# K one batch row further ahead of V in a decode-attention kernel: load order, P V step and buffers moved together

## The chip, the core and the metric

The kernel runs on one core of one Trainium2 chip. The metric is device time in microseconds (us), from the start to the end of one execution; a lower number is better. The profile is one further execution, recorded by the hardware profiler. Its span, from the first to the last instruction, is a little shorter than the device time of the same execution.

The core has five instruction streams that run side by side and meet only through semaphores: TensorE (PE; the weight loads that go with its matmuls are listed as PEld), VectorE (DVE), ScalarE (ACT), GpSimd (POOL) and SyncE (SP). Here SP only issues transfers. Sixteen DMA engines carry them out. Matmul results land in PSUM, all other on-chip data is in SBUF.

## What is computed

One decode step of a transformer layer for 8 batch rows, one token each: a layer norm, attention over the last 2048 positions of a cache, an output projection, and then a small MLP on the sum.

```python
# x: (8, 1, 512); k_cache, v_cache: (8, 8, 8192, 128) bf16; 32 query heads, 8 kv heads
def _A_ref(x, k_cache, v_cache, wq, wo):
    W = 2048                                   # min(4096, max(256, 8192 // 4))
    q = (x @ wq).reshape(8, 1, 32, 128).transpose(0, 2, 1, 3)
    k = jnp.repeat(k_cache[:, :, 8192 - W:, :], 4, axis=1)
    v = jnp.repeat(v_cache[:, :, 8192 - W:, :], 4, axis=1)
    scores = jnp.einsum("bhqd,bhkd->bhqk", q, k) * (128 ** -0.5)
    p = softmax(scores, axis=-1)
    o = jnp.einsum("bhqk,bhkd->bhqd", p, v)
    return o.transpose(0, 2, 1, 3).reshape(8, 1, 4096) @ wo

h  = x + _A_ref(layernorm(x), k_cache, v_cache, wq, wo)
h2 = h + _B_ref(layernorm(h), ...)             # layernorm, gelu(. @ w3) @ w4; the token shift is zero for one token
```

For each batch row the kernel reads 4 MB (in units of 2^20 bytes) of K and 4 MB of V, 64 MB in all, and beside them wq and wo (4 MB each) and the MLP's w3 and w4 (1.75 MB each).

## The kernel before

**Units.** One batch row of K (or V) comes in two transfers of 2 MB, called quads here: quad (k, b, j) holds four kv heads of row b. A *step* p handles a quarter of a quad: `split(i)` turns a step's number into row b = i // 8, quad j and quarter cq. So a row is 8 steps, and 8 rows are 64 steps (`NG`).

**The ring.** All K and V quads go through `ring`, a buffer of 8 slots (`NS`). The list `loads` (lines 235 to 242) gives their order: first row 0 of K, then row 1 of K, then wo, and from there one row of V and one row of K in turn. Quad number n in this list uses slot n % 8. SP issues the transfers in the order of the list (lines 430 to 457), and each waits until the quad eight places before it has been read by PE (`taken`): a K quad by the transposes of its last quarter, a V quad by the P V matmuls of its last quarter. w3 and w4 follow in the places 32 and 33, under the same rule. As SP is one stream, a transfer that waits holds back all behind it.

**A step.** The loop at line 388 writes out the order of PE by hand. In step p PE does: 16 transposes of K (`pe_T`, line 270), whose result ACT and DVE copy from PSUM to SBUF, half each (`evict`, lines 279 and 281); a piece of the softmax of an earlier row, if one is due; the P V matmuls of step p - `LPV` (`pe_PV`, line 360), 16 of them with 16 columns; and the score matmuls of step p - `LQK` (`pe_QK`, line 290). With `LPV` = 16, step p of row b works on V of row b - 2.

**The softmax of row b** starts when its last scores are there, in step 8b + 9: the maximum over a row of scores (`softmax_1`, DVE, line 299), its spread over the heads by two small PE matmuls with DVE work between them (`softmax_2` and `softmax_3`, lines 303 to 316), exp with the row sum on ACT (line 317), the expansion of P by a mask (line 325, on POOL, in the last row on DVE), four groups of transposes of P on PE (`softmax_4`, line 335), each copied to `pT_sb` by DVE (line 340), and the inverse of the sums into `rL` (`softmax_5`, lines 348 and 349). `softmax_5(b)` is called in step 8b + 16, just ahead of the first P V step of row b. `pT_sb` and `rL` have two buffers each, so rows b and b - 2 share one.

**The end.** After 64 steps with transposes come 16 without (`NG + LPV` = 80 in all). In steps 64 to 71 run the P V of row 6 and the softmax of row 7; in steps 72 to 79 the P V of row 7, then `scale` (line 369: times `rL`), the output projection in two halves (`pe_wo`, lines 379 and 383), and the MLP (lines 467 to 532). The last quad of V is loaded in four pieces with a semaphore each, so that the P V of a quarter can start when that quarter has landed. P V adds up in one PSUM tile, `oT_ps`, for all rows (the last half row uses `kbank[1]`); the first P V of a row waits until the row before has been scaled out of it.

## Time and profile before

| | us |
|---|---|
| device time, median of 3 runs | 209.04 (208.78 to 209.84) |
| device time of the profiled execution | 208.47 |
| its span | 206.7 |
| TensorE busy | 162.9 (79% of the span) |
| VectorE busy | 82.5 (40%) |
| ScalarE busy | 79.5 (38%) |
| GpSimd busy | 32.2 (16%) |

The transfers from HBM are 79.18 MB (here in units of 10^6 bytes), 383 GB/s over the span. The times of single instructions, the clock and the state of the DMA engines over the span stand in the prediction, each where it is used. A row of the chain of waits or of the timeline reads: start in us, duration in us, engine and line, what is written and read, and how many instructions were merged. In brackets stands how long the engine was idle before it and what ended that. A row of the DMA issues ends with the time from the issue of a transfer to its landing.

### The profile page before, as it was taken

What the parts mean: (1) busy time and instruction counts of PE and PEld (TensorE: products, weight loads), DVE (VectorE), ACT (ScalarE), POOL (GpSimd) and SP (SyncE); (2) the same over time, 40 slices, a digit from 0 to 9 for tenths busy, and PEclk for the clock granted to TensorE, in tenths of its full rate; (3) what the DMA queues carried; (4) which work ended last, traced back from release to release, by engine and by line L of the source; (5) the groups of instructions that cost most, each with busy time, mean ns of one, the idle gap of its engine ahead of it and who ended that gap; (6) DMA issues with size and microseconds to landing.
All of it is one profiled execution on the core that took longest, in us unless ns stands there. A gap on an engine that the chain in (4) does not pass through costs nothing.

```text
span 206.7 us, 6192 instructions
## 1 busy us (share of the span) xinstructions
PE 162.9 (79%) x2861; PEld 125.2 (61%) x2861; DVE 82.5 (40%) x197; ACT 79.5 (38%) x91; POOL 32.2 (16%) x38
## 2 busy tenths in 40 slices
PE   0047999970059999996999599989996999758885
PEld 0047666540057787784878386867784776457884
DVE  7303545450014346434344425356344444463022
ACT  5002756830013554552355135535552463030021
POOL 7000000430000340070007000700430061000000
PEclk9999999996556999999699969999999999955555
DMA  7999999999999999999999999999999999996000
GB/s 293 419 403 406 453 406 373 383 450 414 444 419 438 422 434 422 428 431 425 431 428 427 431 428 428 431 428 428 431 425 431 428 428 420 405 423 265 17 3 2
DMA packets 10249, 79.57 MB, mean 385 GB/s; under 512 B 744, under 2 KB 4848, under 8 KB 6000
## 3 DMA queue, kind: packets, MB, share of 16 engines
q1 hardware_dynamic: 10208, 79.18, 91.3%
q8 instruction: 22, 0.36, 0.6%
q14 instruction: 3, 0.02, 0.0%
q10 hardware_dynamic: 16, 0.01, 0.0%
HBM read 79.18 MB, written 0.01 MB: 383 GB/s over the span
## 4 chain that ended last, share of the span: by engine, by line
PE 45%; DMA 36%; SPq 12%; DVE 5%; issue 1%; ACT 0%
DMA ring<-in_A_k_cache_dram 30%; PE kT_ps L270 17%; SPq L174 12%; PE S_ps L290 9%; PE oT_ps L360 7%; DMA wbig<-in_A_wq_dram 6%; PE sm L335 2%; PE S_ps L383 2%; PE S_ps L221 2%; PE kT_ps L486 2%; DVE pT_sb L340 1%; DVE P_sb L325 1%; PE sm L348 1%; PE kT_ps L360 1%; PE S_ps L523 1%
## 5 line engine op out<-in xcount | busy, mean ns | idle before, releaser
L279 ACT ACTIVATE kT_sb<-kT_ps 128x1024 bf16<-128x1024 bf16 x64 | 65.4, 1024 | 95.4 <-PE kT_ps L270 95.3
L270 PEld LDWEIGHTS kT_ps<-ident_b,ring 128*128 128x128 bf16 x1024 | 61.8, 102 | 47.3 <-DMA ring<-in_A_k_cache_dram 23.0
L270 PE MATMUL kT_ps<-ident_b,ring 128*128 128x128 bf16 x1024 | 72.8, 228 | 21.5 <-DMA ring<-in_A_k_cache_dram 21.5
L281 DVE COPY kT_sb<-kT_ps 128x1024 bf16<-128x1024 bf16 x64 | 44.3, 692 | 87.8 <-PE kT_ps L270 87.8
L325 POOL TENSOR_TENSOR P_sb<-P_sb,mask_b 128x512 bf16<-128x512 bf16 x28 | 28.2, 1041 | 138.4 <-ACT P_sb L317 138.4
L290 PE MATMUL S_ps<-kT_sb,qwin 128*32 128x512 bf16 x256 | 39.9, 610 | 0.0
L360 PE MATMUL oT_ps<-pT_sb,ring 128*128 128x16 bf16 x960 | 33.1, 171 | 0.0
L360 PEld LDWEIGHTS oT_ps<-pT_sb,ring 128*128 128x128 bf16 x960 | 31.0, 99 | 2.1 <-issue 2.0
L335 PE MATMUL sm<-ident_b,P_sb 128*128 128x128 bf16 x128 | 13.2, 230 | 3.4 <-DVE pT_sb L340 1.6
L340 DVE COPY pT_sb<-sm 128x512 bf16<-128x512 bf16 x32 | 13.4, 418 | 4.7 <-PE sm L335 4.7
L335 PEld LDWEIGHTS sm<-ident_b,P_sb 128*128 128x128 bf16 x128 | 8.6, 102 | 7.4 <-issue 4.1
L317 ACT ACTIVATE P_sb<-S_ps,negcol 128x512 bf16<-128x512 f32 x8 | 5.5, 688 | 7.7 <-DVE negcol L316 7.7
L221 PE MATMUL S_ps<-xlnT,wbig 128*128 128x8 bf16 x128 | 3.6, 168 | 6.2 <-DMA wbig<-in_A_wq_dram 6.2
L290 PEld LDWEIGHTS S_ps<-kT_sb,qwin 128*32 128x32 bf16 x256 | 6.7, 93 | 2.5
L221 PEld LDWEIGHTS S_ps<-xlnT,wbig 128*128 128x128 bf16 x128 | 3.5, 104 | 6.3 <-issue 6.3
L498 ACT ACTIVATE s<-vsum,eps 128x8 f32<-128x8 f32 x1 | 0.3, 301 | 17.1 <-DVE vsum L495 17.1
L299 DVE TENSOR_REDUCE mcol<-S_ps 128x1 f32<-128x512 f32 x8 | 5.5, 690 | 3.3 <-PE S_ps L290 3.3
L211 PE MATMUL sm<-ident_b,xln_b 8*128 8x8 bf16 x4 | 0.3, 174 | 6.5 <-DVE xln_b L195 6.5
L348 PE MATMUL sm<-lsel,ones_f 128*128 128x32 f32 x16 | 3.6, 314 | 1.3 <-DVE lsel L344 1.3
L228 DVE TENSOR_SCALAR qwin<-S_ps 128x32 bf16<-128x32 f32 x8 | 0.9, 182 | 9.2 <-PE S_ps L221 9.2
L348 PEld LDWEIGHTS sm<-lsel,ones_f 128*128 128x128 f32 x16 | 3.1, 241 | 1.8 <-DVE lsel L344 1.8
L211 PEld LDWEIGHTS sm<-ident_b,xln_b 8*128 8x128 bf16 x4 | 0.2, 114 | 6.5 <-DVE xln_b L195 6.5
(71 smaller groups left out, 74.5 us busy)
## 6 DMA issues: line engine op xcount, KB each, us to landing
ring<-in_A_k_cache_dram SPq DMA_DIRECT2D x16, 2048.0 KB, 23.8
ring<-in_A_v_cache_dram SPq DMA_DIRECT2D x15, 2048.0 KB, 18.9
wbig<-in_A_wq_dram SPq DMA_DIRECT2D x1, 4096.0 KB, 12.1
wbig<-in_A_wo_dram SPq DMA_DIRECT2D x4, 1024.0 KB, 17.0
ring<-in_A_v_cache_dram SPq DMA_DIRECT2D x4, 512.0 KB, 24.4
ring<-in_B_w_dram SPq DMA_DIRECT2D x1, 1792.0 KB, 21.9
ring<-in_B_w_dram SPq DMA_DIRECT2D x1, 1280.0 KB, 16.6
ring<-in_B_w_dram SPq DMA_DIRECT2D x1, 512.0 KB, 16.0
```

The costliest lines, as they stand in the source:

```text
L174: e.dma_start(dst, src).then_inc(sem, 16)
L221: ins = e.matmul(S_ps[0][:, h * B:(h + 1) * B], wq_v[:, kc, h * DH:(h + 1) * DH], xlnT[:, kc * B:(kc + 1) * B], start=(kc == 0), stop=(kc ...
L270: ins = e.matmul(kT_ps[i % 2][:, c * 128:(c + 1) * 128], ring[:, s, n * DH:(n + 1) * DH], ident_b[:, :], is_transpose=True)
L279: e_lo[i] = AC.op(lambda e: e.activation(kT_sb[:, i % NKT, 0:1024], kT_ps[i % 2][:, 0:1024], ACT.Copy), e_Tlo[i], e_QK.get(i - NKT))
L281: e_hi[i] = DV.op(lambda e: e.tensor_copy(kT_sb[:, i % NKT, 1024:2048], kT_ps[i % 2][:, 1024:2048]), e_Thi[i], e_QK.get(i - NKT))
L290: ins = e.matmul(S_ps[b % 2][32 * h:32 * (h + 1), :], qwin[:, b, 4 * j + h, w0:w0 + 32], kT_sb[:, i % NKT, :].rearrange("p (x h) -> p h x" ...
L299: e_max[b] = DV.op(lambda e: e.tensor_reduce(mcol[:, :], S_ps[b % 2][:, :], AX.X, ALU.max), e_QK[8 * b + 7], e_mT.get(b - 1))
L325: e_sp[b, r] = eng.op(lambda e, r=r, pb=pb, mb=mb: e.tensor_tensor(P4_sb[:, 128 * r:128 * (r + 1), :], pb, mb, ALU.mult), e_exp[b], e_PT.g ...
L335: ins = e.matmul(pT_ps[:, x * 128:(x + 1) * 128], P4_sb[:, 32 * c:32 * (c + 1), :].rearrange("p k h -> p (k h)"), ident_b[:, :], is_transp ...
L340: e_pT[b, r] = DV.op(lambda e: e.tensor_copy(pT_sb[:, j, 4 * r:4 * (r + 1), :].rearrange("p c n -> p (c n)"), pT_ps[:, :]), e_PT[b, r], e_ ...
L348: e_Lb[b] = PE.op(lambda e: e.matmul(sm[:, LB], ones_f[:, :], lsel[:, :], start=True, stop=True), e_lsel[b], e_pT[b, 3])
L360: ins = e.matmul(dst, ring[:, s, n * DH:(n + 1) * DH], pT_sb[:, b % 2, c, :].rearrange("p (h c j r) -> p c j h r", h=4, c=4, j=2)[:, cq, j ...
```

## The change

Five edits that belong together. `LAG` = 2 replaces a distance of one in the load list: V of row b comes behind K of row b + 2 instead of b + 1. `LPV` goes from 16 to 24, so P V runs three rows' steps behind the scores' row, and the loop has 88 steps instead of 80. `pT_sb` and `rL` get three buffers (`NB3`), and the waits for reuse look three rows back instead of two. The call of `softmax_5` is tied to its own row, `base + 7` (which is step 8b + 16, as before), and no longer to the first P V step.

```diff
-LPV = 16
+LPV = 24
+NB3 = 3
+LAG = 2
...
-        pT_sb = sb([128, 2, 16, 128], dt.bfloat16, "pT_sb")
+        pT_sb = sb([128, NB3, 16, 128], dt.bfloat16, "pT_sb")
...
-        rL = sb([128, 2, H], dt.float32, "rL")
+        rL = sb([128, NB3, H], dt.float32, "rL")
...
         loads = []
-        for b in range(NB + 1):
+        for b in range(NB + LAG):
             if b < NB:
                 loads += [("k", b, 0), ("k", b, 1)]
             if b == 1:
                 loads += [("wo", n, 0) for n in range(4)]
-            if b >= 1:
-                loads += [("v", b - 1, 0), ("v", b - 1, 1)]
+            if b >= LAG:
+                loads += [("v", b - LAG, 0), ("v", b - LAG, 1)]
...
-                pT_sb[:, j, 4 * r:4 * (r + 1), :].rearrange("p c n -> p (c n)"), pT_ps[:, :]),
-                e_PT[b, r], e_PV.get(8 * (b - 2) + 7))
+                pT_sb[:, b % NB3, 4 * r:4 * (r + 1), :].rearrange("p c n -> p (c n)"), pT_ps[:, :]),
+                e_PT[b, r], e_PV.get(8 * (b - NB3) + 7))
...
-            e_rL[b] = DV.op(lambda e: e.reciprocal(rL[:, b % 2, :], sm[:, LB]), e_Lb[b],
-                            e_scale.get((b - 2, 1)))
+            e_rL[b] = DV.op(lambda e: e.reciprocal(rL[:, b % NB3, :], sm[:, LB]), e_Lb[b],
+                            e_scale.get((b - NB3, 1)))
...
                 elif base + 4 <= p <= base + 6:
                     softmax_4(b, p - base - 4)
+                elif p == base + 7:
+                    softmax_5(b)
             i = p - LPV
             if 0 <= i < NG:
                 b, j, cq = split(i)
-                if i % 8 == 0:
-                    softmax_5(b)
```

The readers of `pT_sb` and `rL` in `pe_PV` and `scale` take `b % NB3` in the same way.

More of the change, by code (lines that the diff above doesn't have):

```diff
@@ L360, in f @@
                     ins = e.matmul(dst, ring[:, s, n * DH:(n + 1) * DH],
-                                   pT_sb[:, b % 2, c, :].rearrange("p (h c j r) -> p c j h r", h=4, c=4, j=2)[:, cq, j],
+                                   pT_sb[:, b % NB3, c, :].rearrange("p (h c j r) -> p c j h r", h=4, c=4, j=2)[:, cq, j],
                                    start=(n == 0), stop=(n == NCQ - 1))
@@ L368, in scale @@
             hh = slice(16 * j, 16 * (j + 1))
-            e_scale[b, j] = DV.op(lambda e: e.tensor_tensor(oT_all[:, hh, b], src, rL[:, b % 2, hh], ALU.mult),
+            e_scale[b, j] = DV.op(lambda e: e.tensor_tensor(oT_all[:, hh, b], src, rL[:, b % NB3, hh], ALU.mult),
                                   e_rL[b], *waits)
```

## The prediction

> **What bounds the kernel now.** I read the page's slices of the span first.

> ```profile
> PEclk9999999996556999999699969999999999955555
> DMA  7999999999999999999999999999999999996000
> GB/s 293 419 403 406 453 406 373 383 450 414 444 419 438 422 434 422 428 431 425 431 428 427 431 428 428 431 428 428 431 425 431 428 428 420 405 423 265 17 3 2
> ```

> A slice is 206.7 / 40 = 5.17 us. The DMA engines are full from the second slice to the 36th, about 186 us, mostly at 425 to 431 GB/s; then they empty while the program runs on for 20 us. So there are two parts: a stream of transfers that nothing interrupts, and a tail. The change removes no byte, so what it can change is what is still to be computed when K and V have come. The chain of waits shows what links the two.

> ```profile
> 40.72 18.55 DMA ring<-in_A_k_cache_dram
> ...
> 137.56 20.36 DMA ring<-in_A_k_cache_dram
> 157.92 0.05 issue
> 157.96 1.07 PE kT_ps L270 x16
> ...
> 178.73 0.70 DVE mcol L299
> ...
> 181.89 2.50 DVE P_sb L325 x4
> ...
> 188.31 0.64 PE sm L348 x2
> 188.95 1.69 PE oT_ps L360 x64
> 190.64 0.44 PE kT_ps L360 x16
> 191.11 0.24 DVE oT_all L369
> 191.35 0.05 issue
> ...
> 202.35 1.67 PE S_ps L523 x56
> ```

> PE waits for the first quad of K of row 7 until 157.92. From there PE sets the pace: eight steps with transposes, then the serial softmax of row 7 (178.73 to 188.95), and only then P V of row 7, the projection and the MLP, to 206.7. Everything behind 157.92 is 48.7 us on this path. V of row 7 and w3, w4 come through the stream meanwhile.

> **The change, part by part.** *K in the stream.* Numbered by place among the quads, K of row b stands at places 4b - 2 and 4b - 1 before, and at 4b - 4 and 4b - 3 after (row 1 keeps its places, so this holds from row 2 on). K of row 7 moves from 26, 27 to 24, 25, where V of row 5 was. The DMA issues, taken window by window, show when the old tenants of those places landed.

> ```profile
> 36.49 4.19 SPq L174 DMA_DIRECT2D ring<-in_A_v_cache_dram  x2
> ...
> 128.58 8.94 SPq L174 DMA_DIRECT2D ring<-in_A_v_cache_dram  x2
> 137.56 1.25 SPq L174 DMA_DIRECT2D ring<-in_A_k_cache_dram  x2
> 146.82 12.93 SPq L174 DMA_DIRECT2D ring<-in_A_v_cache_dram  x7
> 166.27 11.14 SPq L174 DMA_DIRECT2D ring<-in_B_w_dram  x3
> ```

> ```profile
> ring<-in_A_v_cache_dram SPq DMA_DIRECT2D x1, 2048.0 KB, 13.0
> ...
> ring<-in_A_v_cache_dram SPq DMA_DIRECT2D x1, 2048.0 KB, 19.6
> ...
> ring<-in_A_v_cache_dram SPq DMA_DIRECT2D x1, 2048.0 KB, 16.1
> ```

> The first is the issue at 36.49: place 4 landed at 49.5, against 40.72 + 18.55 = 59.27 for K of row 2 at place 6. The second is the issue at 128.58: place 24 landed at 148.2, against 157.92 for place 26. Both differences are 9.7 to 9.8 us, so K of row 7 should come 9.7 us sooner. The third is the second quad of that pair, landed at 136.98 + 16.1 = 153.1:

> ```profile
> 136.98 0.54 SPq L174 DMA_DIRECT2D ring<-in_A_v_cache_dram  x1
> ```

> *The gates.* Does SP issue as early as the stream needs it? Before, quad n waits for quad n - 8 as follows: K of row b + 1 for K of row b - 1, V of row b - 1 for P V of row b - 3, both in steps 8b - 5 and 8b - 1. After, K of row b + 1 waits in the same steps, and ahead of it stands V of row b - 2, which waits for P V of row b - 4, with `LPV` = 24 again in steps 8b - 5 and 8b - 1. Two quads of V and two of K are issued per row, at the same steps, in the same order; each K row is preceded by the V that the same step uses. The steps as a whole run two places earlier against the stream, and so do the gates. The distance from gate to landing (16.1 us for the tightest quad of the row) therefore stays. PE could start row 2 at 49.5: its work on row 1 is done at 46, as the wait shows that ends in the first of the following rows of the timeline (59.32 - 13.83 = 45.5). And PE must not fall behind: between the K landings of rows 5, 6 and 7 it has time over.

> ```profile
> 59.32 1.89 PE L270 MATMUL kT_ps<-ident_b,ring 128*128 128x128 bf16 x16 [13.83 <-DMA ring<-in_A_k_cache_dram]
> ...
> 98.22 1.07 PE L270 MATMUL kT_ps<-ident_b,ring 128*128 128x128 bf16 x16 [1.79 <-DMA ring<-in_A_k_cache_dram]
> ...
> 100.39 1.89 PE L270 MATMUL kT_ps<-ident_b,ring 128*128 128x128 bf16 x16
> ...
> 119.12 1.27 PE L270 MATMUL kT_ps<-ident_b,ring 128*128 128x128 bf16 x16 [2.35 <-DMA ring<-in_A_k_cache_dram]
> ...
> 138.51 1.07 PE L270 MATMUL kT_ps<-ident_b,ring 128*128 128x128 bf16 x16 [0.58 <-DMA ring<-in_A_k_cache_dram]
> ```

> It waits 0.58 to 2.35 us for K at these row starts, and in steps 16 to 23 it will have no P V at all. So the 9.7 us reach row 7 undiminished. Term: **-9.7 us**, bounds -9.9 and -9.6 from the spread of the landings.

> *A cold start of row 7.* The same rows show a cost of waiting. Sixteen transposes take 1.07 us, and 1.89 after the long wait; after waits of 1.79 and 2.35 us one slow group follows too (1.89 at 100.39, 1.27 at 119.12 and more behind it), after 0.58 none. Row 7 at 157.96 started with 1.07 and had no slow group. After the change its start is a new draw: nothing, or about 0.9 us (1.89 - 1.07 = 0.82, a little for the other matmuls). This is on the path. I take **+0.5**, bounds 0 and 1.7 (two slow groups). [...]

> *The tail gets eight more steps.* Row 7's softmax has the same place in the steps, with P V of row 5 between its pieces instead of row 6. Row 6's P V, until now hidden between those pieces, moves behind `softmax_5(7)`: PE's order puts it in steps 72 to 79, ahead of row 7's. That is 8 x 16 = 128 matmuls. At the tail's low clock 64 of them took 1.69 us (188.95), so 128 take 3.38 us. Lower bound, at the row's normal pace, and upper, when each step's 16 run alone:

> ```profile
> 161.16 0.38 PE oT_ps L360 x16
> ```

> ```profile
> 186.31 0.62 PE L360 MATMUL oT_ps<-pT_sb,ring 128*128 128x16 bf16 x16
> ```

> 8 x 0.38 = 3.0, 8 x 0.62 = 5.0. I take 1.69 x 2, since the steps stand back to back there. Term: **+3.4 us**.

> *The hand-over of `oT_ps`.* P V of row 7 must wait until row 6 is scaled out. Before, this was done at 186.97 under the softmax:

> ```profile
> 186.97 0.31 DVE L369 TENSOR_TENSOR oT_all<-oT_ps,rL 128x16 bf16<-128x16 f32 x2
> ```

> Now it lies bare: 0.31, plus 0.03 and 0.05 to get to DVE and back (190.64 + 0.44 to 191.11, and the 0.05 at 191.35). Term: **+0.4**, bounds 0.3 and 0.7. Without the cover of the softmax nothing else stands behind it but the tail.

> *At nothing.* The third buffers: rows three apart meet eight steps later, so the waits on `e_PV` and `e_scale` stand to their steps as before. `softmax_5` keeps its step. Row 7 needs no new instruction on SP, ACT or POOL. V of row 7 waits for P V of row 4 (steps 59, 63) instead of K of row 6 (51, 55), and w3 and w4 stand behind it; that is covered by the queue of quads still in flight, and priced as the first rival.

> *The sum.* -9.7 + 0.5 + 3.4 + 0.4 = -5.4 us: the span goes from 206.7 to 201.3. With 208.47 - 206.7 = 1.77 around it the profiled execution would take 203.1; the median of the runs is 0.57 above the profiled one, so 209.04 - 5.4 = **203.6 us**. With all bounds on one side: -9.9 + 0 + 3.0 + 0.3 = -6.6 (202.4), and -9.6 + 1.7 + 5.0 + 0.7 = -2.2 (206.8).

> *What is late next.* P V of row 6 starts at 188.95 - 9.7 + 0.5 = 179.8 and ends at 183.2, row 7's starts at 183.6. The last transfers at their old places in the stream:

> ```profile
> 155.80 0.60 SPq L174 DMA_DIRECT2D ring<-in_A_v_cache_dram  x1
> ...
> 159.13 0.62 SPq L174 DMA_DIRECT2D ring<-in_A_v_cache_dram  x1
> ```

> ```profile
> L174 SPq DMA_DIRECT2D ring<-in_B_w_dram x3: 374/1023/1674, 166.3 to 176.4; - x3
> ```

> ```profile
> ring<-in_A_v_cache_dram SPq DMA_DIRECT2D x1, 2048.0 KB, 23.1
> ...
> ring<-in_A_v_cache_dram SPq DMA_DIRECT2D x1, 512.0 KB, 24.6
> ...
> ring<-in_B_w_dram SPq DMA_DIRECT2D x1, 512.0 KB, 16.0
> ```

> Issue and time to landing give: the first quad of V of row 7 at 155.80 + 23.1 = 178.9; the last piece of the second at 159.13 + 24.6 = 183.7; the end of w4, issued at 176.4 (last start in the summary of its line), at 192.4. V's first quad is there 4.7 us ahead of its use. w4's end, if it stopped the last 16 of 56 matmuls, would allow an end at 192.4 + 0.5 + (206.7 - 202.35 - 1.67) = 195.6, below 201.3. So the stream is the next bound, some 5 us away.

> **The rivals.** *V of row 7 comes late.* Its second quad can be issued only when P V is done in step 63:

> ```profile
> 174.10 0.55 PE L360 MATMUL oT_ps<-pT_sb,ring 128*128 128x16 bf16 x16
> ```

> 9.2 us earlier that ends at 165.4. If the 24.6 us from issue to landing are a property of the transfer, the pieces would land up to 192.5 (165.4 + some 2.5 for four issues of about 0.6 + 24.6). The last sixteen P V matmuls of row 7 would end 0.4 us later, at 192.9, and row 7 be scaled from there; before, that began at 194.78:

> ```profile
> 194.78 0.24 DVE oT_all L369
> ```

> So 209.04 - 1.9 = **207.1**. For it: the gate really moves by eight steps. Against it: issues with a short queue ahead of them landed in 13.0 and 16.1 us, which shows that the 24.6 is queueing; the stream needs the pieces at 180 to 184, 15 us and more after the gate.

> *The stream stalls and K's lead is lost* (the other side). Place: the second V quad of each row, behind whose gate K of the next row stands on SP. If the step's lead made the gates late by a few microseconds, the DMA engines would run dry each row and K would fall back toward its old times, while the eight extra steps of the tail stay. With the lead all gone the time is 209.04 + 3.4 + 0.4 = **212.8**; the point at which there is no gain is a loss of 5.4 us over the five rows from 3 to 7, 1.1 us a row. For it: the ring has no free slot, and 16.1 us from issue to landing is the least in the steady part. Against it: the distance in steps is the same before and after, at 16.1 us the stream showed no gap, and 13.0 was enough once.

> *Part of the lead is lost*, between those: a row of PE time over its K interval, or a stall of about a microsecond a row; then the time stays within about 1 us of **209**. Against it are the waits of 0.58 to 2.35 us.

> **How the numbers follow.** Forecast 0.80 (202.4 to 206.8, likeliest 203.6); V late 0.06 (207.1, still faster by 0.9%); part of the lead lost 0.05; lead lost, slower, 0.09. A measurement of this kernel can tell about 0.5%, 1 us, from no change. So faster 0.86, same 0.05, slower 0.09. The range for 8 in 10 leaves out the last two cases, 0.14, and a little of each end: it runs from 201.8, the lower bound less 0.6 (about what median and profiled run differ by), to 207.1, which takes in the late V.

> **What would show it.** In the profile after: PE's first transposes of row 2 at about 49.5 and of row 7 at 148.2; DMA engines full up to slice 36 or so; the maximum of row 7 at 169.5 instead of 178.73; 128 matmuls of line 360 in a block behind the last line 348, then two line 369 with PE waiting some 0.4 us; w3 and w4 landed by 193. The prediction is wrong if K of row 7 lands later than 151, if DMA share drops between rows, if the P V block takes over 5 us, or if PE waits for V or w3 in the tail.

## The result and the profile after

| | before | after |
|---|---|---|
| device time, median of 4 runs | 209.05 us (208.78 to 209.84) | 206.67 us (205.8 to 206.95) |
| profiled execution | 208.47 us | 206.4 us |
| its span | 206.7 us | 204.6 us |

The ratio is 0.9873, with a 95% interval of 0.9832 to 0.9915. The change makes the kernel 2.4 us faster, where 5.4 us had been forecast. In the changed kernel the line numbers from 32 on are two higher: P V is now line 362, the transposes of K 272, the projection 385.

The slices of the span, after (5.1 us each):

```profile
DMA  7989999999999999999999999999999999998100
GB/s 271 442 375 439 420 432 371 382 438 424 426 432 426 439 426 423 432 426 432 428 426 432 426 420 439 423 439 423 429 426 423 442 423 427 406 419 367 78 3 2
```

The stream is as full as before and thins out at the same time: the engines' share is 0.94 from 186 to 188 us in both kernels, and 0.51 before and 0.56 after from 188 to 190. No gap shows between the rows in these slices, so the ring's gates are met as argued. The start of row 2 on PE, from the timeline, and the chain of waits from row 7 on:

```profile
49.46 1.89 PE L272 MATMUL kT_ps<-ident_b,ring 128*128 128x128 bf16 x16 [3.93 <-DMA ring<-in_A_k_cache_dram]
```

```profile
148.44 0.05 issue
148.49 1.07 PE kT_ps L272 x16
...
169.25 0.70 DVE mcol L301
...
179.02 0.64 PE sm L350 x2
179.66 3.41 PE oT_ps L362 x128
183.07 0.02 issue
183.10 0.32 DVE oT_all L371 x2
183.41 0.14 issue
183.55 0.68 PE oT_ps L362 x20
184.23 0.79 issue
185.02 1.32 PE oT_ps L362 x44
186.34 0.44 PE kT_ps L362 x16
...
187.37 1.80 PE S_ps L385 x64
189.17 2.04 issue
191.21 1.46 PE kT_ps L362 x48
...
200.27 1.67 PE S_ps L525 x56
```

Row 2 starts at 49.46 and row 7 at 148.49, 9.86 and 9.47 us sooner than before. The softmax of row 7 ends 9.29 us sooner (179.02 against 188.31). P V of row 6 is the block of 128 matmuls, 3.41 us, and the hand-over of `oT_ps` takes 0.48 us (183.07 to 183.55). Up to here the change stands 5.4 us ahead: P V of row 7 starts at 183.55 instead of 188.95. Then two rows appear that the tail before did not have: "issue" of 0.79 and of 2.04 us, PE standing still with no releaser that the profile can name. They end the gain at 2.1 us of span.

Do they wait for V of row 7? The issues of the first and the last piece of its second quad, and the time from each to its landing:

```profile
165.20 0.54 SPq L176 DMA_DIRECT2D ring<-in_A_v_cache_dram  x1
...
167.35 0.60 SPq L176 DMA_DIRECT2D ring<-in_A_v_cache_dram  x1
```

```profile
ring<-in_A_v_cache_dram SPq DMA_DIRECT2D x1, 512.0 KB, 14.9
...
ring<-in_A_v_cache_dram SPq DMA_DIRECT2D x1, 512.0 KB, 16.4
```

They landed at 180.1 and 183.75, where the old stream had them. The gate eight steps later cost nothing: the pieces spent 8 to 9 us less in the queue. By these rows V is there 7 us before the second pause ends. But the second pause stands exactly ahead of the matmuls that wait for the second of these pieces, so the rows alone do not settle it. The first pause can't be a wait of the program: it lies 20 matmuls into row 7's P V, and waits are set only every 16.

What the two places share is their distance. From the first pause to the second PE does 44 + 16 + 4 + 64 = 128 matmuls (the 4 are line 381, x into the projection), and each comes with a weight load: 256 instructions. The profile has a queue that carries instructions:

```profile
q8 instruction: 22, 0.36, 0.6%
```

22 packets of 0.36 MB in all are 16.4 KB each. With 2 x 2861 matmuls and weight loads on PE, 22 is one packet for every 260 of them. When the packets of the tail started shows in windows of 0.1 us, at 182.6 and at 188.8:

```profile
q8 instruction: 1, 0.02, 57.6%
...
q8 instruction: 1, 0.02, 60.0%
```

The share is one of 16 engines' time, so the first packet took 0.576 x 16 x 0.1 = 0.92 us on its engine. PE goes on at 185.02 and 191.21: 2.4 us after the packet's start, both times. So a new theory stood against the waiting for V: PE's instructions come in blocks of 256; in the dense tail a block is used up in 3.4 us (128 matmuls, 3.41 us), and its successor, which shares the DMA engines with the stream, comes too late. No row shows what a packet holds: that one packet brings one block of 256 is an estimate from the one packet for every 260 and from the 256 between the two pauses.

### The profile page after: what moved, and what is told of

Same layout as the page of the kernel before. It is cut to its first block, busy times and chain, and to the rows that moved or that the text cites. A ratio compares the mean times of both kernels' runs of the same rounds, so it can differ in the third digit from the quotient of the medians.

```text
span 204.6 us, 6193 instructions
## 1 busy us (share of the span) xinstructions
PE 164.6 (80%) x2861; PEld 126.4 (62%) x2861; DVE 82.5 (40%) x197; ACT 79.4 (39%) x91; POOL 32.2 (16%) x38
## 4 chain that ended last, share of the span: by engine, by line
PE 48%; DMA 42%; DVE 5%; issue 2%; ACT 2%; POOL 1%; SPq 0%
DMA ring<-in_A_k_cache_dram 42%; PE kT_ps L272 20%; PE S_ps L292 9%; PE oT_ps L362 8%; PE sm L337 2%; PE S_ps L385 2%; PE kT_ps L488 2%; DVE P_sb L327 1%; DVE pT_sb L342 1%; PE sm L350 1%; PE kT_ps L362 1%; PE S_ps L525 1%; ACT P_sb L319 1%; PE sm L305 1%; PE sm L315 1%
## 5 line engine op out<-in xcount | busy, mean ns | idle before, releaser
L272 PEld LDWEIGHTS kT_ps<-ident_b,ring 128*128 128x128 bf16 x1024 | 62.7, 103 | 39.6 <-DMA ring<-in_A_k_cache_dram 15.2
L272 PE MATMUL kT_ps<-ident_b,ring 128*128 128x128 bf16 x1024 | 73.7, 230 | 13.8 <-DMA ring<-in_A_k_cache_dram 13.8
L362 PE MATMUL oT_ps<-pT_sb,ring 128*128 128x16 bf16 x960 | 32.3, 171 | 1.3 <-issue 0.8
L362 PEld LDWEIGHTS oT_ps<-pT_sb,ring 128*128 128x128 bf16 x960 | 30.4, 100 | 3.3 <-issue 3.2
L371 DVE TENSOR_TENSOR oT_all<-oT_ps,rL 128x16 bf16<-128x16 f32 x15 | 2.4, 221 | 6.5 <-PE kT_ps L362 3.4
## 6 DMA issues: line engine op xcount, KB each, us to landing
ring<-in_A_k_cache_dram SPq DMA_DIRECT2D x16, 2048.0 KB, 24.8
ring<-in_A_v_cache_dram SPq DMA_DIRECT2D x15, 2048.0 KB, 21.0
ring<-in_A_v_cache_dram SPq DMA_DIRECT2D x4, 512.0 KB, 15.6
ring<-in_B_w_dram SPq DMA_DIRECT2D x1, 512.0 KB, 16.1
```

Source lines behind the costliest of these rows:

```text
L272: ins = e.matmul(kT_ps[i % 2][:, c * 128:(c + 1) * 128], ring[:, s, n * DH:(n + 1) * DH], ident_b[:, :], is_transpose=True)
L362: ins = e.matmul(dst, ring[:, s, n * DH:(n + 1) * DH], pT_sb[:, b % NB3, c, :].rearrange("p (h c j r) -> p c j h r", h=4, c=4, j=2)[:, cq, j],
```

## The experiments

In what was expected, theory F is the fetch of instruction blocks, C the same with the fetch made slow by full DMA engines, L the wait for V. Each time is the median of four executions, and each ratio is to the kernel before, timed beside it.

**64 more matmuls early on PE.**

```diff
+            if p == 16:
+                def pad(e):
+                    for _ in range(64):
+                        ins = e.matmul(oT_ps[:, 256:272], ident_b[:, :], ident_b[:, 0:16], start=True, stop=True)
+                    return ins
+                PE.op(pad)
```

> The changed kernel with 64 more small matmuls on PE ahead of step 16, where PE idles for K anyway; their result is not used. Theory F (PE's instructions come in blocks of 256, that is 128 pairs of weight load and matmul, and PE runs dry at the end of a block while the next is fetched): the two pauses of 0.8 and 2.0 us in the tail move 64 matmuls forward in the program: the first into row 6's P V block after about 84 of its 128 matmuls, the second to about the start of the first half of the projection; in their old places (20 matmuls into row 7's P V, and ahead of its last 48) there is none. Time 205.5 to 207.5. Theory L (the pauses wait for the last quad of V): the pauses stay where they are in the program, PE's last 48 P V matmuls start at 191.2, time 206.7.

Measured: 205.85 us, ratio to the kernel before 0.9822 (0.9771 to 0.9872). PE's timeline in the tail:

```profile
180.68 3.59 PE L362 MATMUL oT_ps<-pT_sb,ring 128*128 128x16 bf16 x128
184.76 1.85 PE L362 MATMUL oT_ps<-pT_sb,ring 128*128 128x16 bf16 x64 [0.49 <-DVE oT_all L371]
...
188.23 1.87 PE L385 MATMUL S_ps<-oT_all,wbig 128*128 128x8 bf16 x64 [0.60 <-issue]
189.96 1.43 PE L362 MATMUL kT_ps<-pT_sb,ring 128*128 128x16 bf16 x48
191.71 0.59 PE L385 MATMUL S_ps<-oT_all,wbig 128*128 128x8 bf16 x16 [0.32 <-DVE oT_all L371]
192.78 1.45 PE L385 MATMUL S_ps<-oT_all,wbig 128*128 128x8 bf16 x48 [0.48 <-issue]
```

The old places are clean: row 7's 64 matmuls run through, and the last 48 follow the projection without a break, though V came no sooner. The pauses have gone to the start of the projection's first half, as F said (64 matmuls ahead of the second old place), and to 16 matmuls into the second half, 128 matmuls further on. The expected one inside row 6's block is missing; the packet for it started at 178.0, still in the softmax, where PE waits for DVE anyway (0.84, 1.12 and 0.67 us of it from 172 to 179 in the changed kernel). L is out: the added matmuls run at 46.5, some 140 us earlier, and the last piece of V lands at 184.2 here, no sooner than the 183.75 of the change. The whole is only 0.8 us faster than the change itself (their intervals overlap), with 1.75 us less of pauses. The rest was lost at row 7's start: one group of 16 transposes took 1.89 us there, and row 6's block begins at 180.68 instead of 179.47 in the same view.

**w3 and w4 cut to three small transfers.** This kernel leaves out most of the MLP's weights; PE's program stays as it is.

```diff
-        dma(SP, w3_sb, B_w3.rearrange("(k p) f -> p k f", p=128), sem_w3, w_free[0])
+        dma(SP, w3_sb[:, 0:1, 0:512], B_w3.rearrange("(k p) f -> p k f", p=128)[:, 0:1, 0:512], sem_w3, w_free[0])
...
+        dma(SP, w4_sb[:, 0, :], w4_src[:, 0, :], sem_w4a,
             w_free[1])
...
+        dma(SP, w4_sb[:, FA, :], w4_src[:, FA, :], sem_w4b)
```

> The changed kernel, but of w3 and w4 only a small part is loaded (three transfers of 128 rows of 1 KB), so the stream of transfers ends about 8 us sooner; the MLP computes with what else lies in the ring. Theory C (the fetch of instructions is slow because the DMA engines are full): the second pause shrinks below 1 us, the first stays; time 204.5 to 205.5. Theory F without contention (a fetch takes over 2 us in any case): both pauses stay, 0.8 and 2.0 us, time 206 to 207. Theory L: both stay, since V stands ahead of w3 and w4 in the stream.

Measured: 204.13 us, 0.9739 (0.969 to 0.9788), 2.5 us below the change.

```profile
183.36 0.68 PE L362 MATMUL oT_ps<-pT_sb,ring 128*128 128x16 bf16 x20 [0.49 <-DVE oT_all L371]
184.99 1.32 PE L362 MATMUL oT_ps<-pT_sb,ring 128*128 128x16 bf16 x44 [0.95 <-issue]
...
187.27 1.86 PE L385 MATMUL S_ps<-oT_all,wbig 128*128 128x8 bf16 x64
188.99 1.44 PE L362 MATMUL kT_ps<-pT_sb,ring 128*128 128x16 bf16 x48
```

The first pause stays (0.95), the second is gone. The program on PE is the same, and V came no sooner (its last piece lands at 184.0), so the second pause needs the bytes of w3 and w4. A table of windows for the changed kernel, and behind it for this run (length, busy time of the engines, clock, DMA share, GB/s):

```profile
186.00:188.00 2.00, 1.66 (x59) 1.56 (x57) 0.23 (x1) 0.00 (x0) 0.00 (x0) 0.50 0.94 391
188.00:190.00 2.00, 1.17 (x44) 1.08 (x41) 0.00 (x0) 0.00 (x0) 0.00 (x0) 0.50 0.56 224
```

```profile
184.00:186.00 2.00, 1.05 (x40) 1.01 (x38) 0.00 (x0) 0.00 (x0) 0.00 (x0) 0.50 0.06 19
186.00:188.00 2.00, 1.67 (x59) 1.56 (x57) 0.23 (x1) 0.00 (x0) 0.00 (x0) 0.50 0.04 12
```

With the engines at 0.04 the block's packet started at 186.4, with them at 0.94 it started at 188.8, at nearly the same point of the tail (the kT_ps matmuls start at 186.17 here, at 186.20 in the changed kernel). With the engines full the packet came 2.4 us later. Counted in blocks of 128 matmuls from the first pause, a block begins at 185.02 in the changed kernel and at 184.99 here, and the packet of the block behind it starts 3.8 and 1.5 us later. This speaks for C.

**Row 6's P V behind the softmax, loads as before.** The one part of the change that was priced as a loss, put alone into the kernel before.

```diff
-        for p in range(NG + LPV):
+        for p in range(NG + LPV + 8):
...
+            if p == 8 * (LAST - 1) + LPV or p == 8 * LAST + LPV:
+                softmax_5((p - LPV) // 8)
             i = p - LPV
+            if p >= 64:
+                i = p - LPV - 8 if p >= 72 else -1
...
-                if i % 8 == 0:
+                if i % 8 == 0 and b < LAST - 1:
```

> The kernel before with one thing of the change alone: P V of row 6 moved behind the softmax of row 7, all loads as before. The tail then runs when the DMA engines are nearly idle. By the terms of the prediction: 3.4 + 0.4 us more than before, 212.9. Theory C: no pause or little ones, 212.9 to 213.5. Theory F: one to three pauses of 0.5 to 2 us in the dense matmuls, 214 to 217. Theory L: 212.9, no pause.

Measured: 212.73 us, 1.0144 (1.0091 to 1.0197). Against the 209.63 of the kernel before, timed beside it, that is 3.1 us, with an interval of about 1.9 to 4.1; the two terms of 3.8 lie in it.

```profile
189.03 3.59 PE L360 MATMUL oT_ps<-pT_sb,ring 128*128 128x16 bf16 x128
193.11 1.85 PE L360 MATMUL oT_ps<-pT_sb,ring 128*128 128x16 bf16 x64 [0.49 <-DVE oT_all L369]
...
195.92 1.86 PE L383 MATMUL S_ps<-oT_all,wbig 128*128 128x8 bf16 x64
197.64 1.43 PE L360 MATMUL kT_ps<-pT_sb,ring 128*128 128x16 bf16 x48
```

The windows of this run, as above:

```profile
188.00:190.00 2.00, 1.42 (x38) 1.42 (x39) 0.88 (x3) 0.00 (x0) 0.00 (x0) 0.50 0.50 211
190.00:192.00 2.00, 2.00 (x82) 2.00 (x79) 0.00 (x0) 0.00 (x0) 0.00 (x0) 0.50 0.25 98
```

The same dense run of matmuls, 9.5 us later, when the stream runs out, has no pause at all. Density alone does not make them; F without contention is out, C stands. The blocks lie at the same places here and begin at 189.59 and 193.64; the packets of the next ones start at 190.4 and 194.4, 0.8 and 0.7 us later. With the 2.4 us from a packet's start to its use, that is sooner than the 4.0 us that a block takes here (189.59 to 193.64).

**Row 6's P V back under the softmax, with the loads of the change.** Two P V steps in each of the steps 64 to 71, row 6 in a PSUM bank of its own.

```diff
+        def pv_steps(p):
+            if NG <= p < NG + 8:
+                return [NG - 24 + 2 * (p - NG), NG - 23 + 2 * (p - NG)]
+            i = p - LPV if p < NG else p - 16
+            return [i] if 0 <= i < NG else []
...
+                elif b == LAST - 1:
+                    dst = kbank[3][:, 16 * j:16 * (j + 1)]
+                    pe_PV(i, dst, e_lo[NG - 1], e_hi[NG - 1], e_lo[NG - 2], e_hi[NG - 2])
```

> The changed kernel with P V of row 5 in steps 64 to 67 and of row 6 in steps 68 to 71, two P V steps in each, so that row 6 runs under the softmax of row 7 again; row 6 adds up in a PSUM bank of its own, and the loop has 80 steps. Theory F or C: the block of 128 matmuls (3.4 us), the hand-over (0.5) and most of the pauses (2.8) leave the path, until the landing of w4 at about 192.4 binds: 199.5 to 202.5. Theory L: the last 48 P V matmuls still start at 191.2, no gain: 206 to 207.

Measured: 202.72 us, 0.9675 (0.9617 to 0.9733), just above the expected range.

```profile
150.58 1.89 PE L272 MATMUL kT_ps<-ident_b,ring 128*128 128x128 bf16 x16
...
181.73 1.88 PE L362 MATMUL oT_ps<-pT_sb,ring 128*128 128x16 bf16 x64
...
187.12 1.43 PE L362 MATMUL kT_ps<-pT_sb,ring 128*128 128x16 bf16 x48 [0.68 <-issue]
```

P V of row 7 starts at 181.73, 1.8 us sooner than in the changed kernel, and the last 48 matmuls at 187.12 instead of 191.21. One pause of 0.68 us is left, ahead of them. The gain is less than the block's 3.4 us and the hand-over for two reasons that the timeline shows: row 7 drew a slow group at its start (1.89), and the doubled P V steps stand ahead of the last score steps, so that the first matmul of the softmax (line 305) starts at 171.79 instead of 169.99.

**The change again, and a better fit.** The same idea with the P V steps dealt out by the gaps that the run with row 6 behind had left bare, and that version once more with the 64 early matmuls.

```diff
+                return take({2: 2, 3: 4, 5: 3, 6: 1, 7: 1}.get(p - NG, 0))
...
+            if p == NG:
+                for i in take(2):
+                    pv(i)
...
+            if p == NG + 1:
+                for i in take(2):
+                    pv(i)
...
+            if p == NG + 7:
+                for i in take(1):
+                    pv(i)
```

> The changed kernel once more, on the chip of the next two runs: 205.5 to 207.2; both pauses at their old places, after 20 matmuls of row 7's P V and ahead of its last 48.

> As the run with row 6 under the softmax, but with the P V steps of rows 5 and 6 dealt out by the gaps of row 7's softmax that the run with row 6 behind showed bare on PE (0.8, 0.6, 1.8, 1.5, 0.5, 0.5, 0.7 us): two ahead of row 6's sums, then the last two score steps first, then 2, 2, 4, 3, 1, 1, 1. The scores of the last step come about 0.9 us sooner and the softmax waits less for PE: 1 to 2 us less than 202.7, so 200.7 to 201.8. Theory C: the pause ahead of the last 48 P V matmuls stays, 0.7 to 2 us, as the tail now lies wholly in the stream. A rival: V of row 6 lands after its new place and holds up the softmax, 202 to 204.

> The one before with 64 more small matmuls ahead of step 16, whose result is not used. Theory C: no pause ahead of the last 48 P V matmuls; pauses, if any, at the start of the first half of the projection and 16 matmuls into the second, under 1 us each; 200.0 to 201.8.

Measured: the change again 206.70 us (0.9839, 0.9791 to 0.9886), with pauses of 0.65 and 1.77 us at the old places. The fitted version **201.46 us, 0.9588 (0.9555 to 0.9622)**, the best of all here. With the early matmuls 202.35 us (0.9638, 0.9601 to 0.9675), slower than the 200.0 to 201.8 expected. PE's timeline of the fitted version, then of that with the early matmuls:

```profile
173.70 1.37 PE L362 MATMUL kT_ps<-pT_sb,ring 128*128 128x16 bf16 x46 [0.80 <-issue]
...
180.17 1.32 PE L362 MATMUL oT_ps<-pT_sb,ring 128*128 128x16 bf16 x44 [0.58 <-issue]
...
186.08 1.45 PE L362 MATMUL kT_ps<-pT_sb,ring 128*128 128x16 bf16 x48 [1.77 <-issue]
```

```profile
174.03 0.59 PE L362 MATMUL kT_ps<-pT_sb,ring 128*128 128x16 bf16 x16 [0.41 <-DMA ring<-in_A_v_cache_dram]
...
176.81 0.20 PE L362 MATMUL kT_ps<-pT_sb,ring 128*128 128x16 bf16 x2 [1.37 <-issue]
...
188.91 1.45 PE L385 MATMUL S_ps<-oT_all,wbig 128*128 128x8 bf16 x48 [2.13 <-issue]
```

Now that P V of row 6 and the tail up to the last 48 P V matmuls lie inside the stream (the loads took 0.84 to 1.18 of the engines' time in each microsecond from 168 to 188), the fitted version has three pauses, 3.15 us together; only the last had been expected. The early matmuls only move them: the place ahead of the last 48 is clean again, but one of 2.13 us, more than twice the most that was expected, stands 16 matmuls into the projection's second half, and one of 1.37 us hits the softmax itself. In this run a P V step also waited 0.41 us for V of row 6, the rival that had been named for the fitted version. Moving the boundary of a block was no cure. Fewer bytes at that time took one pause away (w3 and w4 cut); whether fewer instructions per microsecond would do it was not tried.

Over the first profile of the change and these seven runs, 13 pauses of PE in the softmax of row 7 and the tail ended 2.2 to 2.5 us after the start of a packet in the instruction queue, as here:

```
kernel                         packet starts   PE goes on   apart
the change                     182.6           185.02       2.4
the change                     188.8           191.21       2.4
64 early matmuls               190.5           192.78       2.3
w3, w4 cut                     182.5           184.99       2.5
row 6 under the softmax        184.8           187.12       2.3
fitted                         183.7           186.08       2.4
```

The reverse holds as well. Counted off in blocks of 128 matmuls from the pauses, the nine traces, that of the kernel before among them, have one packet for each block, and it starts only after the block before has begun. Of 191 blocks none begins less than 2.19 us after the start of its packet, and all 13 pauses are among the 17 blocks that begin less than 2.6 us after it. The kernel before was close to a pause too: the packet for its last 48 P V matmuls started at 190.5, 2.8 us before they began.

## Why the prediction went wrong

Term by term, on the profiled executions (span 206.7 to 204.6):

| step of the prediction | predicted, us | measured, us |
|---|---|---|
| K of row 7 sooner | -9.7 | -9.47 (157.96 to 148.49) |
| cold start of row 7 | +0.5 | 0 (group at 150.62: 1.07) |
| softmax of row 7 | 0 | +0.18 (30.35 to 30.53, row 7's start to line 350) |
| row 6's block | +3.4 | +3.41 |
| hand-over of `oT_ps` | +0.4 | +0.48 |
| the tail behind it, unchanged | 0 | +0.47 in row 7's P V, +2.83 in two pauses |
| sum | -5.4 | -2.1 |

The +0.47 are 0.31 in row 7's first 64 matmuls (0.68 + 1.32 against 1.69) and 0.16 in its last 48 (1.46 against 1.30). In the run with row 6 behind, which has the hand-over and no pause, the first 64 take 1.85 and the last 48 take 1.30. So 0.16 of the 0.47 goes with the hand-over, which then costs 0.64 instead of the 0.4 of the sum, and 0.31 appears only where there are pauses.

That the change stands just 5.4 us ahead where P V of row 7 starts, the whole forecast, is partly luck: the 0.5 of the cold start was not drawn, and made up for 0.23 less of K's lead (just outside its bounds of 9.6 to 9.9), 0.18 in the softmax and the rest in row 6's block and the hand-over.

*Right*: the direction, the lead of K that row 2 has and row 7 keeps, the gates that move with the steps, and the two costs that the prediction saw in the tail. The three rivals did not come about: V of row 7 was not late, and no part of K's lead was lost, as row 7's start shows.

The cold start had been taken at half its price, and the changed kernel's draw was the cheap one. The runs with 64 early matmuls and with row 6 under the softmax drew the other: the same group took 1.89 us, and row 6's sums (line 350) came 1.0 us later (167.81 in both against 166.81).

## What to carry to other kernels

A stage moved forward in time runs among other neighbours: ask not only whether its data has landed, but what else it draws from the shared DMA engines there, its own instructions among it: here a packet of the instruction queue started 2.4 us later at a share of 0.94 than at 0.04. PE's pauses lay 128 matmuls with their weight loads apart here. Where many small matmuls follow each other without a wait, count them in such blocks, and see in the instruction queue how long before the block each packet starts: it was 2.2 to 2.5 us ahead of all 13 pauses. And a load order that brings one operand sooner pays in full only if the work it releases does not push other work bare into the tail: here putting row 6's P V back into the gaps of the last softmax gained more than the change itself (206.70 to 201.46 us, timed side by side).

## What was not expected of the hardware

Pauses of 0.5 to 2.1 us on PE at distances of 128 matmuls with their weight loads, shown in the profile as "issue" with no releaser. In these 13 cases the packet started 2.3 to 4.2 us after the block before its own had begun; in the dense matmuls of the run with row 6 behind, which meet shares of 0.50 and less, 0.4 to 0.8 us after. The packets measured above take 0.92 and 0.96 us, yet PE goes on only 2.2 to 2.5 us after their start.

The slow group at a row's start is not a matter of the wait's length alone: in the changed kernel 2.03 us of idle PE ahead of row 7 brought none, in the run with 64 early matmuls 1.67 us brought one. In the kernel before, 1.79 us brought one behind 98.22, and the same 1.79 us none behind 157.96, the start of row 7 there.

```profile
148.49 1.07 PE L272 MATMUL kT_ps<-ident_b,ring 128*128 128x128 bf16 x16 [2.03 <-DMA ring<-in_A_k_cache_dram]
150.62 1.07 PE L272 MATMUL kT_ps<-ident_b,ring 128*128 128x128 bf16 x16
```

```profile
148.60 1.07 PE L272 MATMUL kT_ps<-ident_b,ring 128*128 128x128 bf16 x16 [1.67 <-DMA ring<-in_A_k_cache_dram]
150.74 1.89 PE L272 MATMUL kT_ps<-ident_b,ring 128*128 128x128 bf16 x16
```

What else decides whether a start draws a slow group, no run here shows.
